# Windowed attention and a gated MLP on one core: q, k and the weights loaded and cast by GpSimd's DMA queue, with all steps in a new order

## The chip, the cores and the metric

The kernel runs on one core of a Trainium2 chip. Its engines are TensorE (PE, with weight loads PEld), VectorE (DVE), ScalarE (ACT), GpSimd (POOL) and SyncE (SP, which here only issues DMAs). The metric is the device time of one execution in microseconds.

## The reference, cut to what matters

Inputs and output are f32. There are 8 batches, 8 heads of 64, a sequence of 576, a model width of 512 and a d_ff of 1024.

```python
scores = q @ k.T / sqrt(64)                       # per batch and head
mask = (rel >= 0) & (rel < 64)                    # rel = row - column
attn = softmax(where(mask, scores, -1e9)) @ v
x = attn.transpose(0, 2, 1, 3).reshape(B, S, 512)

h = maximum(x @ w_in, 0)                          # w_in 512 x 1024
u, v = h[..., :512], h[..., 512:]
v_n = (v - mean(v)) / sqrt(var(v) + 1e-6)
v_s = einsum('ts,bsd->btd', w_spatial, v_n) + b_spatial[None, :, None]
out = (u * v_s) @ w_out                           # w_out 512 x 512
```

## The kernel before, in words

All matmuls are in f16, so every f32 input is cast once on its way. The work is cut into steps. A step has a name, an engine and numbered buffers, and the whole order of the program is a table (ORDER) in which each word is one step: `Vr0_2:ACT:0` is the step Vr0_2 on ACT with buffer 0. Each engine does its own steps in the table's order and waits where an input or a buffer isn't ready; `DQ` in a word is SP's DMA queue. No planner runs when the kernel is built.

Attention goes by batch b and group g of four heads.

- `ldk`, `ldq` (L412) load 576 KB of f32 into a staging buffer (tag `nat`, 8 buffers, shared with the weights); `ck`, `cq` (L289 to L300) cast it to f16 on DVE, ACT or POOL; `tk`, `tq` (L419) transpose it on DVE in 32 x 32 blocks.
- `ldv` (L433) loads v in five pieces with runs of 256 bytes; `cv` casts it, and `sl`, `su`, `s4` (L445 to L458) make a copy that is shifted by 64 rows.
- `S` (L479) are the scores on PE, `E` (L486) their exponential on ACT, `M` (L489) the window mask as a minimum on DVE, `Z` (L502) row sums by a matmul with ones, `P` (L514) the product with v, `N` and `n` (L529, L531) the logarithm of the sums and the exponential of its negative on ACT, `X` (L522) their product with `P` on DVE. Names with `_r` are the same for the last 64 rows.

The MLP goes by batch. `V` and `U` are the two halves of x @ w_in on PE; `Vr` and `Ur` (L669, L763) are their rectifiers on ACT; `Vb`, `Va` (L671, L673) the statistics on DVE; `L1`, `L2` the reciprocal root on ACT; `A` (L728) the normalisation on DVE; `G` the spatial matmul and `Ge` (L797, L800) its product with u on DVE; `O` the output matmul, `Oe` (L647) its copy out of PSUM on ACT, and `st` the store on SP. `W` (L378) transposes w_spatial on PE. `D` (L862) are matmuls on scratch data that only keep PE busy at the start: 27 steps, of which two have nine small matmuls and the others two large ones.

The loads of the weights (`ldwin` L326, `ldwsp` L352, `ldb` L362, `ldwo` L395) go through the same queue and the same staging buffers as q and k, with casts (`cwin`, `cwsp`, `cb`, `cwo`) behind them. The mask and the identity are made first of all on POOL and DVE (L244 to L264). A queue has eight completion semaphores, so the ninth DMA of a queue waits until the first has landed.

Of the kernel before, what the change touches and what calls it, by code (L numbers as in the profile page):

```python
# [18 lines left out]
D24:PE:0 ldb:DQ:0 D5:PE:1 D21:PE:2 ldk0_0:DQ:1 ck0_0:DVE:0 tk0_0:DVE:0 D18:PE:3 D2:PE:2 D14:PE:2  # L19
D19:PE:3 D10:PE:0 ldq0_0:DQ:2 ldk0_1:DQ:3 ldv0_00:DQ:0 ldq0_1:DQ:4 ldv0_10:DQ:1 D3:PE:3 ldv0_11:DQ  # L20
cv0_10:POOL:0 ldk1_0:DQ:5 ck0_1:ACT:1 ldv0_12:DQ ldv0_13:DQ ldv0_01:DQ cq0_0:DVE:2 ldq1_0:DQ:6
tq0_0:DVE:1 ldv0_02:DQ D1:PE:2 S0_0:PE:0:1 tk0_1:DVE:2 D22:PE:0 E0_01:ACT:0 E0_00:ACT:1 cq0_1:DVE:3
tq0_1:DVE:3 D15:PE:3 D6:PE:1 D0:PE:2 D26:PE:0 D23:PE:3 S0_r:PE:1:0 E0_r0:ACT:0 E0_r1:ACT cv0_11:POOL
sl0_10:DVE:0 M0_00:DVE ldv0_03:DQ su0_10:DVE M0_01:DVE ck1_0:DVE:0 M0_r:DVE D8:PE:1 Z0_00:PE:2
ldv0_04:DQ ldwin110:DQ:7 ldv0_14:DQ ldwin111:DQ ldwin100:DQ:1 S0_1:PE:1:0 N0_00:ACT:0 E0_11:ACT:2
D16:PE:0 D7:PE:3 E0_10:ACT:3 M0_11:DVE Z0_01:PE:1 Z0_r:PE:2 D4:PE:0 Z0_11:PE:3 N0_r:ACT:1
N0_01:ACT:2 cv0_00:ACT:1 N0_11:ACT:3 ldwin101:DQ su0_11:DVE M0_10:DVE D12:PE:0 Z0_10:PE:2 D20:PE:1
sl0_11:POOL tk1_0:DVE:4 sl0_00:ACT:1 N0_10:ACT:4 n0_11:ACT n0_10:ACT cq1_0:POOL:2 tq1_0:DVE:5
ldq1_1:DQ:2 ldk1_1:DQ:3 P0_10:PE:0 P0_11:PE:3 cwin110:ACT n0_01:ACT D11:PE:1 cv0_01:POOL
ldwin000:DQ:4 ldwin010:DQ:5 ldwin001:DQ ldwin011:DQ ldwsp1:DQ:6 X0_10:DVE:0 su0_00:DVE X0_11:DVE  # L30
n0_00:ACT sl0_01:POOL cb:POOL su0_01:POOL S1_0:PE:0:1 D25:PE:2 D13:PE:1 P0_00:PE:0 X0_00:DVE:1
E1_01:ACT:3 s40_1:ACT P0_01:PE:2 D9:PE:3 cwin111:POOL cwin100:POOL cwin101:POOL ck1_1:POOL:1
s40_0:ACT E1_00:ACT:2 cwin010:POOL X0_01:DVE cwin001:POOL cwin011:POOL V0_2:PE:1 M1_01:DVE
Vr0_2:ACT:0 n0_r:ACT P0_r:PE:3 Z1_01:PE:0 V0_0:PE:2 ldwsp3:DQ:0 M1_00:DVE N1_01:ACT:5 Vr0_0:ACT:1
cq1_1:DVE:3 Z1_00:PE:1 V0_3:PH:0 V0_1:PE:2 N1_00:ACT:4 cwin000:ACT Vr0_3:ACT:2 Vr0_1:ACT:3
ldwsp0:DQ:7 ldwsp4:DQ:1 ldwsp2:DQ:2 cwsp1:POOL:6 ldv1_00:DQ:2 ldq2_0:DQ:3 X0_r:DVE:0 tq1_1:DVE:7
Vb0_2:DVE:0 V0_4:PE:3 tk1_1:DVE:8 S1_1:PE:1:0 cwsp3:POOL:0 cwsp0:POOL:1 Vb0_0:DVE:1 Vb0_3:DVE:2
Vr0_4:ACT:4 Va0_3:DVE Vb0_4:DVE:3 Va0_4:DVE Va0_0:DVE Va0_2:DVE Vb0_1:DVE:4 Va0_1:DVE U0_2:PH:1
U0_3:PH:0 ldk2_0:DQ:4 U0_4:PE:2 ldv1_01:DQ ldv1_02:DQ ldv1_03:DQ E1_11:ACT:1 E1_10:ACT:0 cwsp2:POOL
cq2_0:POOL:0 M1_10:DVE ldv1_10:DQ:3 Ur0_2:ACT:0 L10:ACT:0 ldv1_11:DQ ldv1_12:DQ ldv1_13:DQ L20:ACT  # L40
ldv1_14:DQ ldq2_1:DQ:5 ldv1_04:DQ ldk2_1:DQ:6 ldwo00:DQ:0 ldwo01:DQ Ur0_4:ACT:1 S1_r:PE:0:1
Z1_10:PE:3 U0_0:PE:1 ldwo10:DQ:7 ldwo11:DQ U0_1:PE:2 E1_r0:ACT:0 Ur0_3:ACT:2 E1_r1:ACT Ur0_0:ACT:3
N1_10:ACT:3 A0_0:DVE:0 A0_3:DVE:1 cwsp4:DVE Ur0_1:ACT:4 W1:PE:0 W3:PE:1 W2:PE:3 W0:PE:2 A0_1:DVE:2
A0_4:DVE M1_11:DVE We1:DVE M1_r:DVE n1_00:ACT We2:ACT We3:ACT A0_2:DVE:3 We0:DVE W4:PE:0 ldq3_0:DQ:1
ldk3_0:DQ:2 ldv2_00:DQ:1 ck2_0:POOL:2 We4:DVE D17:PE:3 Z1_11:PE:1 Z1_r:PE:2 G0_0:PH:3 G0_1:PH:0
tq2_0:DVE:2 n1_10:ACT N1_11:ACT:0 tk2_0:DVE:3 Ge0_0:DVE:0 cv1_00:ACT:2 n1_01:ACT sl1_00:POOL:2
n1_11:ACT su1_00:ACT N1_r:ACT:2 cv1_01:POOL Ge0_1:DVE:1 su1_01:DVE G0_3:PH:1 sl1_01:POOL
cv1_10:ACT:3 Ge0_3:DVE:2 cv1_11:DVE S2_0:PE:0:1 P1_01:PE:2 P1_00:PE:3 X1_00:DVE:2 G0_2:PH:0
sl1_10:POOL:3 ldv2_01:DQ ldv2_02:DQ su1_10:ACT sl1_11:ACT E2_01:ACT:3 n1_r:ACT su1_11:POOL
s41_1:POOL P1_10:PE:1 X1_01:DVE P1_11:PE:3 G0_4:PE:2 X1_10:DVE:3 X1_11:DVE U1_1:PH:1 cq2_1:POOL:3  # L50
E2_00:ACT:2 M2_01:DVE Ur1_1:ACT:5 Ge0_4:DVE:3 ck2_1:POOL:1 ldv2_03:DQ V1_2:PH:3 cwo01:POOL
cwo10:POOL cwo11:POOL Ge0_2:DVE:4 M2_00:DVE Z2_01:PE:2 s41_0:ACT Vr1_2:ACT:5 N2_01:ACT:1 U1_2:PH:1
Ur1_2:ACT:3 P1_r:PE:0 V1_1:PH:3 Vr1_1:ACT:6 cq3_0:POOL:0 Z2_00:PE:2 V1_3:PE:1 tq2_1:DVE:4
# [862 lines left out]
```

## Time and profile before

The time is 195.78 us (median of 3 runs, 195.39 to 196.62). The profiled execution has a span of 193.6 us; the execution time of the runs contains some 2 us beside the span.

| | of the span of 193.6 us |
|---|---|
| PE busy | 184.9 us (95%) |
| DVE busy | 163.7 us (85%) |
| ACT busy | 157.1 us (81%) |
| POOL busy | 87.4 us (45%) |
| SP's queue | 42.04 MB, 73.3% of 16 DMA engines |
| first matmul of the MLP | at 23.42 us |
| last matmul ends | at 189.54 us |

Busy shares are averages over stages of different kinds: about 42 us in which the first batch fills the pipeline, some 147 us in which several batches overlap, and the end. The share of PE also holds the scratch matmuls. What a stage is worth is read from its own windows.

### The profile page before, as it was taken

How to read it: one execution, taken by the hardware profiler on the slowest of the kernel's cores; microseconds unless marked ns; L12 is line 12 of the kernel's file. 1: busy time of each engine (PE TensorE's matmuls, PEld its weight loads, DVE VectorE, ACT ScalarE, POOL GpSimd, SP SyncE). 2: the span in 40 equal slices, each digit the busy share in tenths (PEclk: the TensorE clock that was granted, in tenths of full speed). 3: DMA queues.
4: the chain of work that ended last, by engine and by line, in shares of the span. 5: the costliest groups of instructions: out<-in, count | busy, mean ns of one | idle time of the engine just before them, and what ended most of it. 6: DMA issues, size and time to landing. Idle time of an engine off the chain costs nothing.

```text
span 193.6 us, 7606 instructions
## 1 busy us (share of the span) xinstructions
PE 184.9 (95%) x3218; PEld 107.0 (55%) x3218; DVE 163.7 (85%) x304; ACT 157.1 (81%) x282; POOL 87.4 (45%) x161
## 2 busy tenths in 40 slices
...
PEclk9999999999999999999999999999999999999999
...
GB/s 177 373 316 290 391 355 333 168 275 373 242 205 332 261 335 179 149 38 289 367 230 184 310 310 282 196 177 218 306 125 266 22 3 0 224 30 0 135 166 191
DMA packets 50421, 42.73 MB, mean 221 GB/s; under 512 B 39377, under 2 KB 39761, under 8 KB 50386
## 3 DMA queue, kind: packets, MB, share of 16 engines
q1 hardware_dynamic: 50162, 42.04, 73.3%
q8 instruction: 25, 0.41, 0.9%
q10 hardware_dynamic: 224, 0.20, 0.3%
q14 instruction: 10, 0.08, 0.1%
...
## 4 chain that ended last, share of the span: by engine, by line
PE 70%; DVE 13%; ACT 9%; DMA 3%; issue 2%; SPq 1%
PE bank L617 50%; PE bank L614 4%; PE pair L479 4%; PE bank L514 3%; DMA nk<-in_k_dram 3%; PE bank L502 3%; ACT e L486 3%; DVE qT L419 2%; PE bank L702 2%; DVE e L489 2%; DVE kT L419 2%; DVE st L671 2%; DVE g L797 1%; DVE x L522 1%; ACT lz L529 1%
## 5 line engine op out<-in xcount | busy, mean ns | idle before, releaser
L617 PE MATMUL bank<-wspT,vn 128*64 128x512 f16 (+3 forms) x530 | 39.1, 296 | 0.0
L486 ACT ACTIVATE e<-pair 128x1024 f16<-128x1024 f32 x32 | 32.0, 1030 | 1.6 <-PE pair L479 1.4
L797 DVE TENSOR_TENSOR g<-bank,ru 128x512 f16<-128x512 f32 (+1 forms) x36 | 23.3, 654 | 9.4 <-PE bank L617 7.0
L647 ACT COPY ob<-bank 128x512 f32<-128x512 f32 (+1 forms) x38 | 21.9, 591 | 9.7 <-PE bank L617 8.4
L669 ACT ACTIVATE vs<-bank 128x512 f16<-128x512 f32 (+1 forms) x40 | 23.8, 602 | 7.1 <-PE bank L705 5.6
L617 PE MATMUL bank<-x,win 128*64 128x512 f16 (+2 forms) x304 | 29.1, 327 | 0.0
L617 PEld LDWEIGHTS <-vn 128*64 128x64 f16 (+1 forms) x530 | 20.8, 111 | 13.2 <-issue 0.2
L671 DVE BATCH_NORM_STATS2 st<-vs 128x6 f32<-128x512 f16 (+1 forms) x40 | 26.0, 670 | 2.3 <-ACT vs L669 2.2
L298 POOL COPY hs<-hv 64x512 f16<-64x512 f16 (+1 forms) x36 | 20.1, 585 | 16.3 <-ACT hv L292 8.4
L617 PE MATMUL bank<-win,x 128*64 128x512 f16 x216 | 27.0, 379 | 0.0
L617 PE MATMUL bank<-wout,g 128*64 128x512 f16 (+1 forms) x208 | 24.7, 371 | 0.0
L522 DVE TENSOR_TENSOR x<-bank,lz 128x512 f16<-128x512 f32 x32 | 21.2, 684 | 3.5 <-PE bank L514 2.2
L489 DVE TENSOR_TENSOR e<-e,mask 128x1024 f16<-128x1024 f16 x32 | 23.0, 725 | 0.5 <-ACT e L486 0.4
L763 ACT ACTIVATE ru<-bank 128x512 f32<-128x512 f32 (+1 forms) x38 | 21.6, 584 | 1.5 <-PE bank L617 0.8
L295 POOL CAST hk<-nk 128x384 f16<-128x384 f32 x36 | 19.4, 574 | 7.1 <-DMA nk<-in_k_dram 6.7
L529 ACT ACTIVATE lz<-bank 128x512 f32<-128x512 f32 x32 | 19.0, 599 | 1.9 <-PE bank L502 1.6
L298 POOL CAST hv<-nv 128x512 f16<-128x512 f32 x18 | 11.7, 661 | 18.8 <-DMA nv<-in_v_dram 18.7
L419 DVE STREAM_TRANSPOSE kT<-hk 128x576 f32<-128x576 f32 x16 | 19.9, 1241 | 0.2 <-ACT hk L292 0.2
L419 DVE STREAM_TRANSPOSE qT<-hq 128x576 f32<-128x576 f32 x16 | 19.8, 1237 | 0.2
L531 ACT ACTIVATE lz<-lz 128x512 f32<-128x512 f32 x32 | 19.6, 642 | 0.0
L295 POOL CAST hq<-nq 128x384 f16<-128x384 f32 x27 | 14.9, 588 | 10.3 <-DMA nq<-in_q_dram 7.8
L617 PEld LDWEIGHTS <-win 128*64 128x64 f16 x304 | 14.4, 110 | 9.2
...
## 6 DMA issues: line engine op xcount, KB each, us to landing
...
nv<-in_v_dram SPq DMA_DIRECT2D x64, 128.0 KB, 5.9
...
```

Of the source, the lines that this page charges most:

```text
L295: nc.gpsimd.tensor_copy(o[:, n:n + 384], i[:, n:n + 384])
L298: nc.gpsimd.tensor_copy(o[:, lo:hi, :, :], i[:, lo:hi, :, :])
L419: d = add(f"t{name}{b}_{g}", ("DVE", 1.09), key, lambda e: nc.vector.transpose(qt.t[:, :].rearrange("p (i j) -> p j i", j=18), h.t[:, :].b ...
L486: ex = add(f"E{b}_{g}{u}", ("ACT", 0.91), key, lambda e, u=u: nc.scalar.activation(e2[u].t[:, :, :], sc[u].t[:, :, :], AF.Exp, bias=0.0, s ...
L489: mins.append(add(f"M{b}_{g}{u}", ("DVE", 0.65), key, lambda e, u=u: nc.vector.tensor_tensor(e2[u].t[:, :, :], e2[u].t[:, :, :], mask[:, : ...
L522: lambda e, u=u, ob=ob, lz=lz: nc.vector.tensor_tensor(x.t[:, u, :], ob.t[:, :], lz.t[:, :], ALU.mult),
L617: nc.tensor.matmul(o[c:c + 64, :], w[:, c:c + 64], x, start=start, stop=stop)
L647: lambda e: (nc.vector.tensor_copy if last else nc.scalar.copy)(view(), m.t[rows, 0:n]),
L669: rl = add(f"Vr{b}_{j}", ("ACT", 0.49), key, lambda e: nc.scalar.activation(vs.t[0:jn, :], m.t[0:jn, :], AF.Relu), deps=[pv], acq=[vs], us ...
L671: s1 = add(f"Vb{b}_{j}", ("DVE", 0.6), key + 0.02, lambda e: nc.vector.bn_stats(st6.t[0:jn, 0:6], vs.t[0:jn, :]), deps=[rl], acq=[st6], us ...
L763: lambda e, m=m, ru=ru, n=n: nc.scalar.activation(ru.t[:, 0:n], m.t[:, 0:n], AF.Relu), deps=[pu], acq=[ru], uses=[m])))
L797: nc.vector.tensor_tensor(g.t[:, 0:n], m.t[:, 0:n], ru.t[:, 0:n], ALU.mult)
```

## The change

All loads of k, q, w_in, w_spatial, b_spatial and w_out are issued by GpSimd. Such a transfer has an f32 source and an f16 destination, so the cast takes place on the way, straight into `hqk` (k, q), `win`, `wout`, the rows of w_spatial and row 64 of `wspT`. The staging buffers `nat` and the steps ck, cq, cwin, cwsp, cwo and cb are gone. v and the stores stay on SP, and v keeps its f32 staging and its casts. Making keep, mask, identity and the ones row are now steps of the table (`mkeep`, `mmask`, `mrest`, all on POOL). `Vr`, `Ur` and `Oe` may stand on DVE as well as on ACT (7, 7 and 7 of them do, the one of the last step that was there before among them), and `A` on POOL as well as on DVE (22 of 40 do). Buffer counts change: `natv` 4 to 5, `hqk` 4 to 12, `e2` 4 to 5, `vs` 8 to 10, `ru` 6 to 8. There are 19 steps `D`, each of two large matmuls. The table is new throughout.

```diff
-NWARM, NFILL, FILL = 27, 2, 9
-BUFS = {"nat": 8, "natv": 4, "hqk": 4, "qkT": 9, "hv": 4, "hs": 4, "e2": 4, "er": 1, "lz": 6,
+NWARM = len([w for w in ORDER.split() if w[0] == "D"])
+BUFS = {"natv": 5, "hqk": 12, "qkT": 9, "hv": 4, "hs": 4, "e2": 5, "er": 1, "lz": 6,
...
+    def relu(e, o, i):
+        if e == "ACT":
+            nc.scalar.activation(o, i, AF.Relu)
+        else:
+            nc.vector.tensor_scalar_max(o, i, 0.0)
...
+    MK = [add("mkeep", ("POOL", 0.85), -2.0, make_keep)]
+    MK = [add("mmask", [("DVE", 1.7), ("POOL", 2.0)], -1.9, make_mask, deps=MK)]
+    REST = [add("mrest", ("POOL", 1.9), -1.9, make_rest)]
...
+            for r in range(4):
+                WIN[half, r] = add(
+                    f"ldwin{half}{r // 2}{r % 2}", ("POOL", 0.56), key + 0.01 * (4 * (1 - half) + r),
+                    lambda e, r=r, cs=cs: nc.gpsimd.dma_start(
+                        w_in_sb[r][:, cs], moe_w_in[128 * r:128 * r + 128, cs]), nbytes=0.80, n=128)
...
         def one(name, src, key):
-            n = buf("nat", f"n{name}{b}_{g}")
-            ld = add(f"ld{name}{b}_{g}", ("DQ", 0.45), key, lambda e: nc.sync.dma_start(
-                n.t[:, :], src[b, 4 * g:4 * g + 4, :, :].rearrange("h (i j) d -> (h i) (j d)", j=18)),
-                acq=[n], nbytes=1.57, n=128)
             h = buf("hqk", f"h{name}{b}_{g}")
-            c = add(f"c{name}{b}_{g}", cost(1152), key,
-                    lambda e: cp(e, h.t[:, :], n.t[:, :]), deps=[ld], acq=[h], uses=[n])
+            c = add(f"ld{name}{b}_{g}", ("POOL", 0.56), key, lambda e: nc.gpsimd.dma_start(
+                h.t[:, :], src[b, 4 * g:4 * g + 4, :, :].rearrange("h (i j) d -> (h i) (j d)", j=18)),
+                acq=[h], nbytes=1.57, n=128)
...
-        rl = add(f"Vr{b}_{j}", ("ACT", 0.49), key, lambda e: nc.scalar.activation(
-            vs.t[0:jn, :], m.t[0:jn, :], AF.Relu), deps=[pv], acq=[vs], uses=[m])
+        rl = add(f"Vr{b}_{j}", [("ACT", 0.49), ("DVE", 0.61)], key, lambda e: relu(
+            e, vs.t[0:jn, :], m.t[0:jn, :]), deps=[pv], acq=[vs], uses=[m])
...
-            AP.append(add(f"A{b}_{j}", ("DVE", 0.33), key + 0.2, emit_A,
+            AP.append(add(f"A{b}_{j}", [("DVE", 0.33), ("POOL", 0.7)], key + 0.2, emit_A,
```

**SP's queue at the start.** Before, SP issues the loads of b_spatial (wsb), k (nk), q (nq) and v (nv) of batch 0 and of k and w_in (wi) in turn.

```order
L362 DMA wsb<-in_moe_b_spatial_dram 1x576
L412 DMA nk_0_125<-in_k_dram 128x1152
L412 DMA nq_0_141<-in_q_dram 128x1152
L412 DMA nk_1_143<-in_k_dram 128x1152
L433 DMA nv_0_145<-in_v_dram 128x4x64
L412 DMA nq_1_147<-in_q_dram 128x1152
L433 DMA nv_1_149<-in_v_dram 128x4x64 x2
L412 DMA nk_0_156<-in_k_dram 128x1152
L433 DMA nv_1_149<-in_v_dram 128x4x64 x2
L433 DMA nv_0_145<-in_v_dram 128x4x64
L412 DMA nq_0_165<-in_q_dram 128x1152
```

Now SP issues v alone, and behind v of batch 0 (nv_1_123, nv_0_308) come at once v of batch 1 (nv_1_768, nv_0_875) and of the first group of batch 2 (nv_0_977).

```order
L416 DMA nv_1_123<-in_v_dram 128x4x64 x2
L416 DMA nv_0_308<-in_v_dram 128x4x64
L416 DMA nv_1_123<-in_v_dram 128x4x64
L416 DMA nv_1_123<-in_v_dram 64x4x64
...
L416 DMA nv_0_308<-in_v_dram 64x4x64
L416 DMA nv_1_768<-in_v_dram 128x4x64 x4
L416 DMA nv_0_875<-in_v_dram 128x4x64 x4
L416 DMA nv_1_768<-in_v_dram 64x4x64
L416 DMA nv_0_977<-in_v_dram 128x4x64
```

In the order before, v of batch 1 stood behind all of w_in and w_spatial; now the two kinds of loads stand in different queues, with nothing that holds one for the other.

**POOL at the start.** Before, POOL makes the mask's corner (L244 on), waits for v and casts (hv, hs, hq are v, its shifted copy and q in f16). Now it issues loads (hk, hq are k and q of batches 0 and 1, win is w_in), makes the mask between them, and has two casts of v (the rows hv) in the row, of which the second waits for v of group 0; behind that stand k and q of batch 1's second group and the second half of w_in.

```order
L398 DMA hk_1_129<-in_k_dram 128x1152
L302 MEMSET keep 128x64
...
L398 DMA hq_1_201<-in_q_dram 128x1152
...
L280 CAST hv_1_303<-nv_1_123 128x512 [waits DMAHW1_49,DMAHW0_49]
L358 DMA wspT_100<-in_moe_b_spatial_dram 1x16x36
L398 DMA hq_0_314<-in_q_dram 128x1152
L398 DMA hk_0_316<-in_k_dram 128x1152
L335 DMA win_88<-in_moe_w_in_dram 128x512
...
L280 CAST hv_0_328<-nv_0_308 128x512 [waits DMAHW5_49,DMAHW0_49]
L398 DMA hk_1_370<-in_k_dram 128x1152 [waits DMASW3_49]
```

The casts of k, q and weights are gone from this row, and the loads that other engines wait for now stand in it.

**ACT at the start.** Before (hk is k in f16, e and er the exponentials, lz the sums and their inverses, hv and hs v and its shifted copy, win w_in):

```order
L292 CAST hk_1_158<-nk_1_143 128x1152
L486 ACTIVATE e_0_01_233<-pair_68 128x1024
...
L486 ACTIVATE e_0_11_359<-pair_67 128x1024
L486 ACTIVATE e_0_10_365<-pair_68 128x1024
L529 ACTIVATE lz_r<-bank_71 128x256
L529 ACTIVATE lz_01_383<-bank_70 128x512
L292 CAST hv_0_385<-nv_0_145 128x512
```

Now:

```order
L469 ACTIVATE e_0_10_306<-pair_68 128x1024
L272 CAST hs_1_311<-nv_1_123 64x256
L469 ACTIVATE e_0_11_319<-pair_67 128x1024
L512 ACTIVATE lz_r<-bank_70 128x256
L512 ACTIVATE lz_00_351<-bank_69 128x512
L272 CAST hs_0_332<-nv_0_308 64x256
L272 COPY hs_0_332<-hv_0_328 64x512
L512 ACTIVATE lz_11_375<-bank_72 128x512
```

The cast of k and the casts of w_in are gone; two pieces of v's shifted copy (hs) that need v as it was loaded, and one that needs the cast on POOL (hv_0_328), stand between the exponentials and the logarithms.

**DVE at the end.** Before, the last five products with u (g) stand in a row, and the last copies out of PSUM (ob) behind them:

```order
L797 TENSOR_TENSOR g_2_4828<-bank_70,ru_2_4758 128x512
L797 TENSOR_TENSOR g_3_4871<-bank_69,ru_3_4700 128x512
L800 TENSOR_TENSOR g_4_4896<-bank_72,ru_4_4619 128x256
L835 COPY ob_2_4894<-bank_72 128x256
L647 COPY ob_4_4940<-bank_71 128x256
```

Now the one of the last 64 rows (g_4) comes behind one of those copies:

```order
L780 TENSOR_TENSOR g_0_4769<-bank_71,ru_0_4591 128x512
L780 TENSOR_TENSOR g_3_4773<-bank_70,ru_3_4771 128x512
L818 COPY ob_2_4796<-bank_70 128x256
L783 TENSOR_TENSOR g_4_4862<-bank_69,ru_4_4467 128x256
L818 COPY ob_2_4796<-bank_72 128x256
```

On PE the last spatial matmul, G7_4, moved with it: before it directly followed G7_3, now three output matmuls and half of a fourth stand between them, and G7_3 is followed at once by output matmuls.

More of the change, by code (lines that the diff above doesn't have):

```diff
@@ L18 @@
 ORDER = """
[L19 to L53, printed above, removed]
@@ new lines @@
+ldv0_14:DQ ldq1_0:POOL:4 ldk1_0:POOL:5 s40_1:ACT E0_11:ACT:3 ldv0_03:DQ ldv0_13:DQ ldwin100:POOL
+ldwin111:POOL ldv0_01:DQ su0_10:DVE cv0_11:DVE cv0_00:DVE:1 ldv0_02:DQ M0_10:DVE sl0_00:DVE:1
+M0_11:DVE ldwin101:POOL ldv0_04:DQ su0_00:DVE tq1_0:DVE:4 su0_11:DVE Z0_00:PE:0 Z0_r:PE:1 N0_r:ACT:0
+N0_00:ACT:1 ldwin110:POOL cv0_01:POOL Z0_01:PE:2 D16:PE:3 D17:PE:3 D18:PE:3 Z0_11:PE:3 Z0_10:PE:1
+ldk1_1:POOL:6 sl0_01:POOL s40_0:ACT su0_01:ACT N0_11:ACT:2 n0_00:ACT N0_01:ACT:3 N0_10:ACT:4
+sl0_11:POOL n0_r:ACT P0_01:PE:0 P0_00:PE:3 tk1_0:DVE:5 P0_11:PE:2 ldq1_1:POOL:7 ldwin000:POOL
```

322 lines of the change are left out of this document (159 added, 163 removed).

## The prediction

> **What bounds the kernel now.** I read the page's totals first, then the stages by windows, then TensorE's row of instructions around the stages' borders.
>
> ```profile
> span 193.6 us, 7606 instructions
> PE 184.9 (95%) x3218; PEld 107.0 (55%) x3218; DVE 163.7 (85%) x304; ACT 157.1 (81%) x282; POOL 87.4 (45%) x161
> ...
> PEclk9999999999999999999999999999999999999999
> ```
>
> PE is busy for 95% of the span, and the clock row shows no throttled slice. The windows (us, busy time of PE, PEld, DVE, ACT and POOL, clock, DMA share, GB/s) say where the other 5% lie.
>
> ```profile
> 0.00:9.26 9.26, 6.87 (x21) 2.53 (x22) 6.05 (x16) 2.34 (x2) 2.31 (x11) 1.00 0.78 275
> 9.26:23.42 14.16, 13.17 (x298) 6.76 (x298) 13.29 (x19) 11.82 (x21) 8.60 (x13) 1.00 1.11 329
> 23.42:42.04 18.62, 17.75 (x214) 8.73 (x215) 17.82 (x34) 17.22 (x35) 12.47 (x19) 1.00 0.97 282
> 42.04:189.54 147.50, 147.12 (x2689) 88.95 (x2687) 126.48 (x237) 125.33 (x226) 64.00 (x118) 1.00 0.69 201
> 189.54:193.60 4.06, 0.00 (x0) 0.00 (x0) 0.08 (x1) 0.37 (x1) 0.00 (x0) 1.00 0.54 169
> ```
>
> From 42.04 to 189.54 PE is busy for 147.12 of 147.50 us, and none of it is scratch work (all steps D lie before). PE bounds this stage; DVE, ACT and POOL have 21 us and more to spare in it. The change takes no matmul of the result away, so these 147.1 us stay, and faster casts are worth nothing there. What can move is the first 42 us, where PE's busy time is filled up with scratch matmuls and the DMA engines are full, and the last few.
>
> ```profile
> 1.27 6.87 PE L862 MATMUL bank<-scratch 128*128 128x512 f16 x20 [1.27 <-DVE scratch L237]
> ...
> 13.89 0.67 PE L479 MATMUL pair<-qT,kT 32*128 32x128 f16 x56
> ...
> 23.42 0.39 PE L614 MATMUL bank<-win,x 128*128 128x512 f16 x1
> 24.02 0.82 PE L614 MATMUL bank<-win,x 128*128 128x512 f16 x3 [0.21 <-DVE x L522]
> ...
> 29.85 0.67 PE L479 MATMUL pair<-qT,kT 32*128 32x128 f16 x56 [0.42 <-DVE kT L419]
> 30.45 1.92 PE L617 MATMUL bank<-x,win 128*64 128x512 f16 x16
> 32.30 0.64 PE L614 MATMUL bank<-x,win 128*128 128x64 f16 x16
> ...
> 35.48 2.39 PE L378 MATMUL bank<-id,wn 128*128 128x128 f16 x25
> 37.80 0.61 PE L862 MATMUL bank<-scratch 128*128 128x512 f16 x2
> ...
> 38.69 3.42 PE L617 MATMUL bank<-wspT,vn 128*64 128x512 f16 x30
> ```
>
> Two marks: 23.42, when the first V may start because the attention of batch 0 is done, and 42.04, from where PE is never short. Between them PE has, by distances of starts, nine groups V and U at about 0.9 (30.45 to 32.30 is two: 1.85), U0_4 0.57, W 2.32 (35.48 to 37.80), three G 3.35 (38.69 to 42.04), S1_1 0.60, and Z, S_r, P_r and Z_r at some 1.2 together: about 16 of 18.62 us. So about 2.7 us of that stage is waiting, scratch work included.
>
> **The change part by part, the start.** What stands ahead of 23.42 is a chain of DMA, cast, transpose, scores, exponential. DVE's rows, then ACT's:
>
> ```profile
> 5.26 0.76 DVE L300 CAST hk<-nk 128x1152 f16<-128x1152 f32 x1 [1.66 <-DMA nk<-in_k_dram]
> 6.06 1.26 DVE L419 STREAM_TRANSPOSE kT<-hk 128x576 f32<-128x576 f32 x1
> 7.16 0.75 DVE L300 CAST hq<-nq 128x1152 f16<-128x1152 f32 x1
> ...
> 10.49 0.74 DVE L300 CAST hq<-nq 128x1152 f16<-128x1152 f32 x1
> ...
> 22.67 1.29 DVE L522 TENSOR_TENSOR x<-bank,lz 128x512 f16<-128x512 f32 x2 [0.18 <-PE bank L514]
> ...
> 25.60 1.06 DVE L300 CAST hq<-nq 128x1152 f16<-128x1152 f32 x1
> ```
>
> ```profile
> 8.20 1.15 ACT L292 CAST hk<-nk 128x1152 f16<-128x1152 f32 x1 [6.11 <-DMA nk<-in_k_dram]
> ...
> 14.79 1.94 ACT L486 ACTIVATE e<-pair 128x1024 f16<-128x1024 f32 x2 [0.20 <-PE pair L479]
> ...
> 17.51 0.61 ACT L292 CAST hv<-nv 128x512 f16<-128x512 f32 x1
> 18.02 0.61 ACT L529 ACTIVATE lz<-bank 128x512 f32<-128x512 f32 x1
> 18.65 0.40 ACT L292 COPY hs<-hv 64x256 f16<-64x256 f16 x1
> ...
> 20.61 0.61 ACT L292 CAST win<-wi 128x512 f16<-128x512 f32 x1
> 21.12 1.15 ACT L531 ACTIVATE lz<-lz 128x512 f32<-128x512 f32 x2
> 22.17 1.01 ACT L486 ACTIVATE e<-pair 128x1024 f16<-128x1024 f32 x1
> 23.20 0.71 ACT L292 CAST hs<-nv 64x256 f16<-64x256 f32 x2
> ```
>
> Gone ahead of S0_1 are three casts on DVE (0.76, 0.75, 0.74) and one on ACT (1.15). The four loads, not DVE, then set the pace. SP's issue rows:
>
> ```profile
> 1.21 0.38 SPq L412 DMA_DIRECT2D nk<-in_k_dram  x1
> ...
> 6.14 3.98 SPq L433 DMA_DIRECT2D nv<-in_v_dram  x3
> ...
> 27.08 0.43 SPq L433 DMA_DIRECT2D nv<-in_v_dram  x1
> ```
>
> The first k needed 4.05 us from its issue at 1.21 to its cast at 5.26. What an issue by GpSimd costs the trace does not show. Bounds: SP's 0.38 below, and above the 1.33 that SP's v rows took apiece when the queue was full (3.98 for 3). I take the middle, 0.8, since a row on the engine itself is nearer to compute. Nor is a transfer with a cast shown: below, its time is that of the plain one (half the bytes written); above, it is twice, which is a rival. With plain speed the four 576 KB loads (2.36 MB) share the DMA engines with v of batch 0, which now has a queue to itself. At 329 GB/s of the window, 2.36 MB and half of v's 1.18 take 9.0 us; from about 2 us on that is 11.0 for the fourth load. The transpose (a distance of 1.1 in DVE's rows, 6.06 to 7.16) ends near 12.1, and S0_1 follows near 13.4, against 13.89. The distance before was 1.5 (the cast at 10.49, 0.74 and 1.1 make 12.4), with Z0_00 and its wait for M0_00 ahead of S0_1; that goes, and I take 1.3, since S0_r and its exponentials stay.
>
> From S0_1 to E is 0.90 (13.89 to 14.79), so E starts at 14.3. Before, ACT's list from there to the last inverse took 7.38 (14.79 to 22.17). Out of it go cv 0.51 (17.51 to 18.02), sl 0.40 and cwin 0.51 (20.61 to 21.12); into it come two pieces s4 of 0.37 (half of 23.20's pair, rounded up), su at 0.51 as cv, and n_r at half of what one n takes in 21.12's pair, 0.3: 7.5. Then the last X takes 0.65 (22.67's two at 1.29), and V may have run up to 0.55 of its four matmuls before it: 14.3 + 7.5 + 0.65 - 0.55 = 21.9. To that I add 1.3 of stalls: ACT's two s4 and su stand in front of logarithms and wait for v and POOL's cast, and DVE's cv0_11 and cv0_00 wait for v in front of M0_10 and M0_11. Bounds of this term: 0, if v comes first, and 2.5, worked out under the rivals. The mark comes to **23.2 instead of 23.42: -0.2**.
>
> Of the work between the marks, P_r (0.13) and V0_4 (0.88) now stand ahead of V0_3 and fall into ACT's time: **-1.0**. Of 2.7 us of waiting, the transposes of k1_1 and q1_1 no longer stand behind the cast of 1.06 at 25.60 (PE waited 0.42 for it at 29.85), and the casts of w_spatial between the load and W are gone; waits for the statistics and for A0_1, now on POOL, stay. I take 1.3 left, **-1.4**; bounds 0.5 and 2.7.
>
> **The rest.** Of ACT's 157 us, casts, 14 rectifiers and copies go, some 23; DVE loses and gains about as much; POOL trades 35 casts for 22 A and 50 issues. In the long stage all that is covered by PE: at nothing, while buffers keep their lead. If POOL ran late with A, G would wait: A costs 0.42 on DVE, and on POOL between 0.6 and 1.1, as POOL's cast rows of the same elements:
>
> ```profile
> 11.50 0.61 POOL L300 CAST hv<-nv 128x512 f16<-128x512 f32 x1 [8.33 <-DMA nv<-in_v_dram]
> 14.08 0.92 POOL L300 CAST hv<-nv 128x512 f16<-128x512 f32 x1 [1.97 <-DMA nv<-in_v_dram]
> ```
>
> Four A, two on POOL at 0.9, are ready about as early as five at 0.42. The end:
>
> ```profile
> 185.11 0.69 DVE L797 TENSOR_TENSOR g<-bank,ru 128x512 f16<-128x512 f32 x1 [0.39 <-PE bank L617]
> ```
>
> G7_4 used to run while DVE did the last Ge7_3 of 0.69; now O7_0 follows G7_3 and waits for earlier Ge. The other O7 cover part. I take **+0.5**, between 0 and 0.7. The copy and store after the last matmul are the same: the last window's 4.06.
>
> Sum: 193.6 - 0.2 - 1.0 - 1.4 + 0.5 = 191.5 of span. The median of 195.78 lies 2.2 above the profiled span: 193.7, which I give as 193.6.
>
> A rule of the Trainium skill speaks against the change. The row first: the two casts on POOL above are alike, and the second took 0.92 instead of 0.61 beside a DVE cast, so the two engines do hold each other up, by 0.31. The Trainium skill ("SBUF — State Buffer", SBUF: two separate sides) says that DVE's fast copy modes lock GpSimd out of a port pair, so that it can't write the descriptors of its DMAs meanwhile, and gives 620 ns growing to 3100 ns for such a DMA. By that rule each load issued beside such a DVE copy would come later by up to the copy; no run here shows it for a load.
>
> **The rivals.** *First, v comes late (no change).* v has 256-byte runs, and its queue now competes with big transfers. For: v rows took 1.33 of issue each at a full queue, and the DMA share is 1.11 in that window. Against: v has no k, q or weights ahead of it in its own queue now. Then the stall is 2.5 instead of 1.3 (two pieces of v's 1.18 MB at half of 329 GB/s more, 0.2 MB: 1.2), and POOL's cv0_01 holds k1_1, q1_1 and w_in's second half behind it, so that 0.7 less of the waiting goes: 193.6 + 1.2 + 0.7 = 195.5.
>
> *Second, v of batches 1 and 2 comes first (slower).* SP now issues 1.77 MB of v right behind batch 0's, which before came at 27.08, behind w_in and w_spatial. The start is full: 1.11 and 0.97 of the DMA engines. At 320 GB/s 1.77 MB take 5.5 us. If a share f of it gets ahead of w_in's second half and w_spatial, U0 and W wait by 5.5 f, less some 0.5 of slack that U0 has. 193.6 + 5.5 f - 0.5 is even with before at f = 0.5, over 1% slower from 0.84, and 198.6 at f = 1. For: nothing but the eight semaphores holds SP back. Against: those let only eight v pieces be under way, and each of 128 KB landed 5.9 us after issue. The Trainium skill ("DMA: Bandwidth & Descriptors", Queues, rings and completion order) says that a DMA engine takes its queues in turn, a packet from each; by that rule f would be large, since v's queue never empties early.
>
> ```profile
> nv<-in_v_dram SPq DMA_DIRECT2D x64, 128.0 KB, 5.9
> ```
>
> *Third, loads with a cast are slow (slower).* At half speed, k, q and weights (23.6 of 42 MB) would raise the long stage's share from 0.69 to 0.69 x (1 + 23.6 / 42) = 1.08: DMA would bound it, and 8% of 147.5 is 12 us: 205. Held up for less, it gives 200. Against: 12 buffers for k and q give three batches of lead.
>
> **How the numbers follow.** Within 1% (193.8 to 197.7) is what this kernel's measurement can't tell from no change. The forecast case gets 0.50; its bounds make it 191.0 to 195.2, and since 193.6 is near the border, 0.36 of it is faster, 0.14 the same. The first rival gets 0.22 (0.05, 0.14, and 0.03 slower), the second 0.19 (0.05 the same, 0.14 slower), the third 0.09, all slower. That is 0.41, 0.33 and 0.26. The range 191.2 to 198.6 leaves out the third rival, 0.03 above the second and 0.06 below.
>
> **What would show it.** Right: V starts at about 23.2 with fewer scratch matmuls, PE has no gap from some 39.5 on, and the last matmul ends 2 us earlier. First rival: ACT's hs or DVE's hv rows idle for v. Second: U's first matmuls wait for win, or W for w_spatial, behind landings of v. Third: GpSimd's loads land much later after their issue than the first k's 4.05 and v's 5.9, and k's transposes wait in the long stage. The forecast is wrong if PE waits for A on POOL in the long stage.

## The result, and the profile after

The changed kernel takes 232.01 us (median of 4 runs, 229.82 to 240.53) against 195.69 us (195.39 to 196.62): a ratio of 1.1735, with a 95% interval of 1.1691 to 1.1778. The forecast was 193.6, with a range to 198.6. All ratios below go by the runs within 1.5% of their kernel's fastest, so a median over all runs can lie above its ratio.

The page of the changed kernel, beside the one of before: the span is 34.1 us longer. PE is idle for 36.7 us of it instead of 8.7. Its matmuls on real data, the same in both kernels, take 180.0 us instead of 168.8 (the mean granted clock is 0.962 instead of 1.000), and the scratch matmuls take 10.9 instead of 16.1.

```profile
span 227.7 us, 7662 instructions
## 1 busy us (share of the span) xinstructions
PE 191.0 (84%) x3295; PEld 110.4 (48%) x3295; DVE 163.0 (72%) x288; ACT 138.3 (61%) x249; POOL 124.7 (55%) x171
...
PE   7591898599995999599957999976999799499692
...
PEclk9999599979999999999997999997999999999999
```

PE's row had a 9 in nearly every slice before; now it has 4, 5 and 7 all along the span, and behind some of them the granted clock is lowered. Its windows say that this is not a matter of the start alone (us, busy time of PE, PEld, DVE, ACT and POOL, clock, DMA share, GB/s).

```profile
0.00:42.00 42.00, 31.41 (x463) 16.10 (x463) 27.11 (x50) 22.21 (x39) 22.68 (x47) 0.92 0.97 178
42.00:60.00 18.00, 15.01 (x311) 8.94 (x312) 14.47 (x21) 12.56 (x23) 16.66 (x27) 0.91 0.76 121
60.00:180.00 120.00, 106.13 (x1984) 63.62 (x1980) 98.54 (x173) 86.19 (x155) 74.65 (x94) 0.97 0.65 144
180.00:230.00 50.00, 38.41 (x548) 21.75 (x542) 22.90 (x48) 17.37 (x34) 10.77 (x5) 0.97 0.24 83
```

In the long stage, which had 0.38 us of idle time in 147.5 before, PE is idle for 13.9 of 120 us between 60 and 180. Over the whole span, the waits name one cause for more than half of the idle time (us in total, times, longest):

```profile
PEld L600 <- POOL vn L711: 24.7, 11, 4.2
PE bank L600 <- POOL vn L711: 20.3, 11, 3.7
```

L711 is the normalisation A, and L600 here the spatial matmul G, which reads all five tiles of a batch. The row of L711 by engine (ns: least, median, most):

```profile
L711 POOL TENSOR_SCALAR vn<-vs,mv,ln x22: 2062/2069/2720, 38.4 to 211.9; 128x512 f16<-128x512 f16 x18, 64x512 f16<-64x512 f16 x4
L711 DVE TENSOR_SCALAR vn<-vs,mv,ln x18: 396/413/806, 38.3 to 210.7; 128x512 f16<-128x512 f16 x14, 64x512 f16<-64x512 f16 x4
```

On POOL an A takes 2.07 us, five times DVE's 0.41. Its least and its median are alike, so this is its own price and no disturbance by DVE. POOL as a whole is busy for only 55% of the span: G waits not because POOL is full, but because the last A of a batch ends late. Batch 0 shows it, on POOL's timeline and then on PE's:

```profile
20.74 1.09 POOL L280 CAST hv<-nv 128x512 f16<-128x512 f32 x1 [8.93 <-DMA nv<-in_v_dram]
...
38.45 2.23 POOL L711 TENSOR_SCALAR vn<-vs,mv,ln 128x512 f16<-128x512 f16 x1 [5.01 <-ACT ln L701]
40.64 0.62 POOL L398 DMA_DIRECT2D hq<-in_q_dram  x1
41.31 4.25 POOL L711 TENSOR_SCALAR vn<-vs,mv,ln 64x512 f16<-64x512 f16 x2
```

```profile
10.70 0.67 PE L462 MATMUL pair<-qT,kT 32*128 32x128 f16 x56 [2.48 <-DVE qT L402]
...
16.29 1.47 PE L844 MATMUL bank<-scratch 128*128 128x512 f16 x6
22.69 1.07 PE L485 MATMUL bank<-e,ones 128*64 128x512 f16 x4 [4.93 <-DVE e L472]
...
28.02 0.64 PE L600 MATMUL bank<-win,x 128*64 128x512 f16 x1
...
45.62 2.28 PE L600 MATMUL bank<-wspT,vn 128*64 128x512 f16 x48 [2.79 <-POOL vn L711]
```

Batch 0's three A on POOL run from 38.45 to 45.56, with a load of q between them. Two matmuls of G0 run at 42.44; the others wait until 45.62. There is a second, smaller loss ahead of it: v of batch 0's second pieces (group 0) is there only at 20.7 (POOL's cast waited 8.93 us for it). DVE's casts of v stand in front of M0_10, so PE is idle for 4.93 us before the next row sums; the matmuls behind that pause run at 0.63 us where the same ones took 0.38 before, in the slices whose granted clock is 5 and 9. The scores began at 10.70 instead of 9.26, the first V at 27.6 instead of 23.42.

### The profile page after: what moved, and what is told of

The parts are those of the page before. It is cut to its first block, busy times and chain, and to the rows that moved or that the text cites. A ratio compares the mean times of both kernels' runs of the same rounds, so it can differ in the third digit from the quotient of the medians.

```text
span 227.7 us, 7662 instructions
## 1 busy us (share of the span) xinstructions
PE 191.0 (84%) x3295; PEld 110.4 (48%) x3295; DVE 163.0 (72%) x288; ACT 138.3 (61%) x249; POOL 124.7 (55%) x171
## 3 DMA queue, kind: packets, MB, share of 16 engines
q1 hardware_dynamic: 43168, 18.68, 31.8%
q0 software_dynamic: 7024, 11.68, 30.7%
## 4 chain that ended last, share of the span: by engine, by line
PE 32%; POOL 19%; SPq 11%; DVE 11%; issue 10%; DMA 8%; ACT 6%; POOLq 1%; DVEq 0%; ACTq 0%
PE bank L600 24%; POOL vn L711 18%; SPq L416 10%; DMA nv<-in_v_dram 8%; DVE x L505 2%; PE bank L685 2%; PE pair L462 2%; PE bank L497 2%; DVE g L780 1%; DVE st L654 1%; ACT lz L512 1%; PE bank L485 1%; DVE qT L402 1%; DVE e L472 1%; DVE kT L402 1%
## 5 line engine op out<-in xcount | busy, mean ns | idle before, releaser
L711 POOL TENSOR_SCALAR vn<-vs,mv,ln 128x512 f16<-128x512 f16 (+1 forms) x22 | 47.9, 2181 | 62.5 <-ACT ln L701 47.9
L600 PE MATMUL bank<-wspT,vn 128*64 128x64 f16 (+3 forms) x640 | 48.3, 303 | 20.4 <-POOL vn L711 20.3
L600 PEld LDWEIGHTS <-vn 128*64 128x64 f16 (+1 forms) x640 | 25.3, 121 | 39.8 <-POOL vn L711 24.7
L469 ACT ACTIVATE e<-pair 128x1024 f16<-128x1024 f32 x32 | 32.2, 1026 | 15.6 <-PE pair L462 15.5
L600 PE MATMUL bank<-win,x 128*64 128x512 f16 x240 | 31.8, 383 | 0.2 <-DVE x L505 0.2
L600 PE MATMUL bank<-x,win 128*64 128x512 f16 (+2 forms) x352 | 31.7, 317 | 0.1
L600 PE MATMUL bank<-wout,g 128*64 128x512 f16 (+1 forms) x240 | 28.8, 373 | 0.2
L272 ACT COPY ob<-bank 128x512 f32<-128x512 f32 (+2 forms) x34 | 19.3, 580 | 14.3 <-PE bank L600 9.8
L284 ACT ACTIVATE vs<-bank 128x512 f16<-128x512 f32 (+1 forms) x33 | 19.3, 595 | 10.2 <-PE bank L600 3.0
L284 ACT ACTIVATE ru<-bank 128x512 f32<-128x512 f32 (+1 forms) x31 | 17.8, 586 | 11.5 <-PE bank L600 11.3
L472 DVE TENSOR_TENSOR e<-e,mask 128x1024 f16<-128x1024 f16 x32 | 22.6, 715 | 0.0
L600 PEld LDWEIGHTS <-win 128*64 128x64 f16 x352 | 16.2, 110 | 10.4 <-issue 0.8
L600 PEld LDWEIGHTS <-x 128*64 128x64 f16 x240 | 14.1, 110 | 11.4 <-DVE x L505 1.1
L600 PEld LDWEIGHTS <-g 128*64 128x64 f16 x240 | 13.9, 110 | 10.4 <-DVE g L780 1.0
```

What stands on the lines that cost most here:

```text
L284: nc.scalar.activation(o, i, AF.Relu)
L469: ex = add(f"E{b}_{g}{u}", ("ACT", 0.91), key, lambda e, u=u: nc.scalar.activation(e2[u].t[:, :, :], sc[u].t[:, :, :], AF.Exp, bias=0.0, s ...
L472: mins.append(add(f"M{b}_{g}{u}", ("DVE", 0.65), key, lambda e, u=u: nc.vector.tensor_tensor(e2[u].t[:, :, :], e2[u].t[:, :, :], mask[:, : ...
L600: nc.tensor.matmul(o[c:c + 64, :], w[:, c:c + 64], x, start=start, stop=stop)
L711: ENG[e].tensor_scalar(o[0:jn, :], VS[j].t[0:jn, :], mv_t[b % NSB][0:jn, j, 0:1], ln.t[0:jn, 5 + j:6 + j], ALU.subtract, ALU.mult)
```

## The experiments

Three explanations were to be told apart: the price of A on POOL; the loads, now in two queues; and the new order as such.

**A back on DVE, in the changed kernel.** All 22 words, of this kind:

```diff
-A0_2:POOL:0
+A0_2:DVE:0
```

> The changed kernel with one edit: the 22 normalisations A that stand on POOL go back to DVE, at the same places in the order. Theory 1 (A on POOL is the main cost: 2.07 us each there against 0.41 on DVE, and TensorE's rows wait 20.3 + some 5 us for it): the time falls from 232 by 25 to 32 us, to 200 to 207, and TensorE no longer waits for vn. Theory 2 (the loads at the start and v's late arrival are the main cost): it falls by less than 12 us, to over 220. Theory 3 (the new order as a whole is bad, wherever A stands): over 215, with the waits spread over other rows.

208.5 us, ratio 1.0595 (1.0513 to 1.0678). The fall from 1.1735 is 0.114, some 22 us of the 34: the first theory's direction, a little less than its numbers. 12 us are left.

**A on POOL, in the kernel before.** The same 22 steps:

```diff
-A0_2:DVE:3
+A0_2:POOL:3
```

> The kernel before with one edit: the same 22 normalisations A go from DVE to POOL, at their places in the order before. Theory 1: it slows by 20 us or more, to 215 to 230, since each A takes about 2.1 us on POOL and G waits for the last of a batch. Theory 2: DVE is relieved and POOL had time to spare, so under 200. It also shows whether A's 2.07 us come with POOL's loads: about 2.07 here too if the operation itself costs that, under 1.1 if issuing loads was what slowed it.

229.4 us, ratio 1.1709 (1.1621 to 1.1797). Alone, with nothing else of the change, A on POOL costs as much as the whole change did. The rows of A in this kernel:

```profile
L728 POOL TENSOR_SCALAR vn<-vs,mv,ln x22: 2064/2068/2720, 37.5 to 214.7; 128x512 f16<-128x512 f16 x18, 64x512 f16<-64x512 f16 x4
L728 DVE TENSOR_SCALAR vn<-vs,mv,ln x18: 312/402/791, 33.9 to 213.5; 128x512 f16<-128x512 f16 x14, 64x512 f16<-64x512 f16 x4
```

The 2.07 us are there without a single load issued on POOL, so issuing has nothing to do with it. 22 times the difference of 1.66 is 36.5 us, near the 33.4 that were added, but the time isn't added up tile by tile: in this trace PE's idle time goes from 8.7 to 31.1 us, and its busy time from 184.9 to 198.4 for the same matmuls, at a mean granted clock of 0.937. In the changed kernel the same 22 steps were worth some 22 us.

**What in A is slow on POOL.** One run of the changed kernel with other forms in four batches:

```diff
+                if e == "POOL" and b == 1:
+                    nc.gpsimd.tensor_scalar(o[0:jn, :], i_, m_, None, ALU.subtract)
+                elif e == "POOL" and b == 2:
+                    nc.gpsimd.tensor_scalar(o[0:jn, :], i_, 0.5, 2.0, ALU.subtract, ALU.mult)
+                elif e == "POOL" and b == 3:
+                    nc.gpsimd.tensor_scalar(o[0:jn, :], i_, 2.0, None, ALU.mult)
+                elif e == "POOL" and b == 4:
+                    nc.gpsimd.tensor_copy(o[0:jn, :], i_)
```

> The changed kernel, in which A on POOL has another form in some batches, to price its parts: batch 1 only subtracts (one operand per row), batch 2 subtracts and multiplies by constants, batch 3 multiplies by a constant, batch 4 copies; the others as they were, at 2.07. So the normalisation of batches 1 to 4 is in part left out here, and the time is read only by these rows. If the two operands per row are what costs, batch 2 is near the 0.6 of POOL's copies; if two operations on POOL cost that, batch 2 is near 2.07 and batches 1 and 3 near 1.1; if any tensor with scalars is slow, batch 3 is far over the copy of batch 4.

The rows by form (L721 as it was, L713 batch 1, L715 batch 2, L717 batch 3, L719 batch 4; ns: least, median, most):

```profile
L721 POOL TENSOR_SCALAR vn<-vs,mv,ln x12: 2061/2072/2684, 37.5 to 204.0; 128x512 f16<-128x512 f16 x9, 64x512 f16<-64x512 f16 x3
L717 POOL TENSOR_SCALAR vn<-vs x3: 1501/1626/1802, 109.3 to 113.0; 128x512 f16<-128x512 f16 x2, 64x512 f16<-64x512 f16 x1
L719 POOL COPY vn<-vs x3: 611/612/617, 133.1 to 137.1; 128x512 f16<-128x512 f16 x3
...
L713 POOL TENSOR_SCALAR vn<-vs,mv x2: 1560/1568/1577, 66.3 to 67.9; 128x512 f16<-128x512 f16 x2
L715 POOL TENSOR_SCALAR vn<-vs x2: 1920/1988/2057, 79.2 to 81.2; 128x512 f16<-128x512 f16 x2
```

The third guess is right, by two or three tiles of each form: a tensor with scalars is slow on POOL as such, 1.5 to 1.8 us with one operation and 1.9 to 2.1 with two, whether the scalars are constants or one per row, where a copy of the same tile takes 0.61.

**v of batches 1 and 2 held back, A on DVE.** v of batch 1 uses batch 0's staging buffers, and its words stand behind the casts that free them:

```diff
-ldv1_10:DQ:2 ... ldv1_00:DQ:3
+ldv1_10:DQ:0 ... ldv1_00:DQ:1
```

> The changed kernel with A on DVE as in the first run of this group, and v of batches 1 and 2 held back: v of batch 1 uses the staging buffers of batch 0 and its loads stand behind the casts that free these, with v of batch 2's first group behind them. If v ahead of time takes the bandwidth from v of batch 0's second group, w_in and w_spatial at the start (V began some 4 us later than before in the changed kernel), it is 3 to 5 us faster than the run with A on DVE alone, and the first V starts at about 24 instead of about 28. If the bandwidth of the start isn't what is short, it is within 1 us of that run, or slower, because v of batch 1 then comes late.

209.7 us, ratio 1.0673 (1.0609 to 1.0737): no gain. POOL's cast shows why:

```profile
20.95 1.09 POOL L280 CAST hv<-nv 128x512 f16<-128x512 f32 x1 [8.99 <-DMA nv<-in_v_dram]
```

v of batch 0 is as late with nothing behind it in its queue. The second rival of the prediction, v ahead of its time, is not it.

**v of batch 0 first, A on DVE.** POOL's cast cv0_01, which waits for v, goes ahead of six loads:

```diff
+cv0_01:POOL ldq1_0:POOL:4 ldk1_0:POOL:5 ldwin100:POOL ldwin111:POOL ldwin101:POOL ldwin110:POOL
```

> A on DVE as before this, and one more edit: GpSimd issues k and q of batch 1's first group and the first half of w_in only behind its cast of v of batch 0's second pieces, so these 2.2 MB no longer share the DMA engines with v of batch 0. In the runs with A on DVE v of batch 0 was there at about 20.4 us, with or without v of batch 1 behind it. If the loads of the other queue hold v back, v is there at about 14 to 16, DVE's cast of it waits less, the first V starts 3 to 4 us earlier than 27.4 and the time falls from 208.5 to about 204 to 206. If v's own 256-byte runs or SP's issue set its time, v stays near 20 and the time rises by the later w_in, to 210 to 213.

205.07 us, ratio 1.0441 (1.0362 to 1.0520). POOL's timeline and PE's:

```profile
14.31 0.83 POOL L280 CAST hv<-nv 128x512 f16<-128x512 f32 x1 [6.44 <-DMA nv<-in_v_dram]
15.10 0.57 POOL L398 DMA_DIRECT2D hq<-in_q_dram  x1
```

```profile
18.77 0.62 PE L485 MATMUL bank<-e,ones 128*64 128x512 f16 x4 [1.21 <-DVE e L472]
...
24.81 1.04 PE L685 MATMUL bank<-win,x 128*64 128x512 f16 x2
```

v comes 6 us earlier, PE waits 1.21 instead of 4.93, and the first V starts at 24.8 instead of 27.4. In time that is 3.4 us by the medians (the two intervals just touch). So k and q of batch 1 and w_in, 2.2 MB that are needed later, had taken the DMA engines from v: with two queues the order in which loads were issued no longer is the order in which they land.

**The rectifiers and copies back on ACT.** On top of that, the 19 steps of this kind:

```diff
-Vr0_4:DVE:0
+Vr0_4:ACT:0
```

> The run with A on DVE and v of batch 0 first, with one more edit: the 19 rectifiers and output copies of batches 0 to 7 that the change put on DVE go back to ACT, at the same places. That run is still some 9 us slower than before, with TensorE idle for some 3.5 us between 60 and 180 us (0.3 before) and no cast left on DVE but v's. If the work put on DVE (each about 0.65 there) is what delays others in its row, the idle time falls below 1.5 us and the time by 2 to 4 us, to 201 to 203. If the rows' order as such is what costs, it stays at 204 to 206; if ACT's row can't take it, over 206.

208.03 us, ratio 1.0521 (1.0452 to 1.0590): no gain. Relieving DVE alone doesn't mend the new order. Whether DVE's load costs nothing, or ACT, with 19 steps more, loses what DVE gains, this run doesn't tell.

**The new order with A on POOL at the price of a copy.** POOL's 22 A are plain copies; in the second run v of batch 0 comes first as well.

```diff
+                if e == "POOL":
+                    nc.gpsimd.tensor_copy(o[0:jn, :], VS[j].t[0:jn, :])
+                    return
```

> The changed kernel with POOL's 22 normalisations replaced by plain copies of the same size (0.61 us each in the run of the forms, against 2.07), everything else and every place in the order kept: the new order at the price that the prediction took for A on POOL. The normalisation of these 22 tiles is left out, and with it POOL's wait for the batch's statistics, so this is the best that the order could do. If the price of A is what failed, the time is at most that of the run with A on DVE, 203 to 208. If A's place in POOL's row, behind loads and casts that wait, costs besides, it is 212 or more.

> The same with v of batch 0 first, as in the run with A on DVE and v first (205). If what is left there (some 9 us over before) comes from A standing on DVE, which the new order had not left room for, this comes to 195 to 199; if the new order is slow by itself, 201 to 205, with TensorE's idle time between 60 and 180 us still at 2 us or more.

205.11 us, ratio 1.0382 (1.0297 to 1.0468), and 202.06, ratio 1.0333 (1.0278 to 1.0388). At the price of a copy, and without the wait for the batch's statistics, A on POOL costs no more than on DVE (1.0382 against 1.0595, and 1.0333 against 1.0441 with v first). And yet the new order is 3.3% slower than the old one at its best. The windows from 60 us on, of the run with A on DVE and v first, then of the second one here, then of the kernel before:

```profile
60.00:180.00 120.00, 116.61 (x2216) 72.74 (x2212) 110.86 (x208) 89.65 (x161) 42.03 (x71) 1.00 0.63 142
180.00:230.00 50.00, 17.25 (x202) 9.43 (x198) 7.89 (x18) 7.61 (x15) 0.00 (x0) 0.96 0.17 58
```

```profile
60.00:180.00 120.00, 118.44 (x2237) 77.10 (x2235) 107.13 (x194) 90.77 (x166) 51.77 (x89) 1.00 0.63 143
180.00:230.00 50.00, 15.10 (x182) 9.39 (x178) 7.10 (x15) 6.55 (x14) 0.00 (x0) 0.98 0.17 58
```

```profile
60.00:180.00 120.00, 119.67 (x2172) 72.63 (x2161) 105.42 (x198) 104.86 (x189) 52.81 (x98) 1.00 0.66 189
180.00:230.00 50.00, 9.54 (x136) 5.89 (x130) 3.95 (x7) 4.02 (x8) 0.00 (x0) 0.98 0.15 48
```

Between 60 and 180 us that is 3.4 and 1.6 us of idle time, against 0.3 before. But the greater part is lost earlier. The matmuls that are left at 60 us take 133.9 and 133.5 us (116.61 + 17.25 and 118.44 + 15.10), against 129.2 before. So of the 7.8 us by which the first span is longer (201.4), 4.7 are lost before 60 us, and of the 5.7 of the second (199.3), 4.3.

**The loads alone.** The order before, with the loads of k, q and weights by GpSimd at their old places, without their casts:

```diff
-ldk0_0:DQ:1 ck0_0:DVE:0 tk0_0:DVE:0
+ldk0_0:POOL:0 tk0_0:DVE:0
```

> The loads alone: the order before, with all rectifiers, copies and normalisations on their engines, but k, q and the weights loaded and cast by GpSimd in the places where their loads stood, the casts gone, 12 buffers for k and q, and the mask made on POOL between the first loads. If casting in the transfer costs no transfer time (the changed kernel's trace: 69.9 us of all 16 engines for these loads, as many as the difference of the two kernels' rows gives for before), and v ahead costs little, 192 to 196. If v of batch 1 ahead of w_in and w_spatial costs at the start, 197 to 201. If issuing on POOL holds POOL up, over 201, with waits for POOL's casts and copies of v in the long stage.

199.96 us, ratio 1.0131 (1.0044 to 1.0219). Its longest wait of PE in the first 42 us is one that the rewriting made, POOL's shifted copies of v standing behind eight issues:

```profile
26.72 0.26 PE L498 MATMUL bank<-e,hs 128*64 128x64 f16 x2 [3.19 <-POOL hs L281]
```

From 60 us on this run is as full as the kernel before:

```profile
60.00:180.00 120.00, 119.65 (x2209) 72.22 (x2205) 104.31 (x196) 103.54 (x190) 42.65 (x74) 1.00 0.62 145
180.00:230.00 50.00, 14.53 (x182) 8.55 (x176) 7.76 (x19) 6.87 (x15) 0.00 (x0) 0.97 0.15 48
```

134.2 us of matmuls are left at 60, against 129.2 before. That is all of the 5.0 us by which its span is longer (198.6).

So these copies were put ahead, and identity and ones earlier:

```diff
+cv0_01:POOL sl0_01:POOL su0_01:POOL ldwin000:POOL ldwin010:POOL
```

> The loads alone, in the order before, with one place mended: POOL makes identity and ones early, where it waits for v anyway, and makes the shifted copies of v of group 0 right behind its cast, ahead of the second half of w_in and w_spatial. In the first run of the loads alone TensorE waited 3.5 us for these copies, which stood behind eight issues. If that wait was what made it 4 us slower than before, 196 to 197; if it is v's late arrival (20.8 us) and w_in's (issued from 16.9 on), 199 to 201, with the wait moved to win or v.

Ratio 1.0028 (0.9987 to 1.0069): at its best, no change. But the ten runs lie between 195.24 and 201.11, with a median of 198.27, where the kernel before has 195.92. The kept trace is of the run of 201.11. PE's timeline, and a window:

```profile
10.22 0.67 PE L463 MATMUL pair<-qT,kT 32*128 32x128 f16 x56 [2.34 <-DVE qT L403]
...
23.77 0.39 PE L598 MATMUL bank<-win,x 128*128 128x512 f16 x1
...
47.70 0.27 PE L498 MATMUL bank<-e,hs 128*64 128x64 f16 x2 [2.64 <-ACT hs L273]
```

```profile
42.00:60.00 18.00, 14.87 (x296) 8.64 (x286) 12.16 (x21) 10.87 (x18) 4.15 (x8) 0.81 0.82 162
```

The scores begin 1 us later than before and the first V 0.35 later, though three casts on DVE and some on ACT are gone. But the scores that stand at 42.04 before start at 41.80 here, so up to there nothing is lost. What this run loses, it loses next: v of batch 1, in SP's queue, is late. DVE's cast of it waits 3.90 us, until 46.57, PE waits 3.1 us in two pieces for the shifted copies, and its granted clock is 0.81 in the window. So a queue that is left to v alone doesn't bring v in time here, which is the second case of the expectation. Whether the other runs of this kernel that took longer lost their time there too, no trace shows.

**All loads of the start in one queue.** v of batches 0 and 1 by GpSimd too:

```diff
-                           lambda e, c=c, sn=sn: nc.sync.dma_start(
+                           lambda e, c=c, sn=sn: ENG[e].dma_start(
```

> The loads alone with all loads of the start in one queue: v of batches 0 and 1 is issued by GpSimd too, at the places that its loads had in SP's queue before, the mask is made on DVE, and POOL's first casts of v stand behind the issues. If it is the second queue that breaks the order in which loads arrive, v of batch 0 is there by about 14, the first V starts near 24 and the time is 195 to 198. If GpSimd's way of loading is itself late (the first k took 5.4 us from its issue instead of 4.05) or its issues of v with 512 runs each cost POOL far more than 0.55, the scores start no earlier than 10.4 and the time is 200 or more.

202.8 us, ratio 1.0258 (1.0216 to 1.0300). It answers another question than it was made for. In the kept trace, of the run of 209.10, the scores began at 9.30, as early as before. But POOL was busy with 18 issues, and waits between them for loads to land, until its first cast of v at 17.76. On DVE a shifted copy waited for this cast, with the product with the mask (M) behind it, and PE waited 6.04 us for M.

```profile
20.03 0.64 PE L487 MATMUL bank<-e,ones 128*64 128x512 f16 x2 [6.04 <-DVE e L474]
```

An issue of v took 0.75 there, one of k or q 0.55. Whether one queue brings v in time can't be told from it: the last piece of v of batch 0 was issued only at 17.13, after POOL had waited 1.55 us for an earlier one to land.

**A mixture.** The order before; k and q of batch 0 by SP with casts, all other k and q and the weights by GpSimd:

```diff
+            if b == 0:
+                n = buf("nat", f"n{name}{b}_{g}")
+                ld = add(f"ld{name}{b}_{g}", ("DQ", 0.45), key, lambda e: nc.sync.dma_start(n.t[:, :], rows),
+                         acq=[n], nbytes=1.57, n=128)
...
+            else:
+                c = add(f"ld{name}{b}_{g}", ("POOL", 0.56), key,
+                        lambda e: nc.gpsimd.dma_start(h.t[:, :], rows), acq=[h], nbytes=1.57, n=128)
```

> A mixture meant to beat the kernel before: its order, with k and q of batch 0 loaded by SP and cast on DVE and ACT as before, and k and q of the other batches and all weights loaded and cast by GpSimd, with POOL's row mended as in the run with the shifted copies first. In the runs with the loads alone the first scores began about 1 us later than before (10.2 against 9.26), since GpSimd's first loads land later, and the first V 0.35 us later, though ACT had three casts less ahead of it. If the late first loads are the only price of the loads, this starts V at 22.8 to 23.2 and gives 194.5 to 195.3, 0.3 to 0.7% faster than before. If v and w_in are as late as in those runs, it is the same as before, 195.5 to 197.

194.84 us (12 runs), ratio 0.9940 (0.9916 to 0.9964): 0.6% faster than the kernel before, which is little but clear of the noise. PE's timeline and the long stage:

```profile
8.68 0.67 PE L471 MATMUL pair<-qT,kT 32*128 32x128 f16 x56 [1.43 <-DVE qT L411]
...
22.85 0.39 PE L606 MATMUL bank<-win,x 128*128 128x512 f16 x1
```

```profile
60.00:180.00 120.00, 119.65 (x2159) 72.55 (x2156) 103.13 (x196) 101.27 (x185) 43.25 (x74) 1.00 0.61 142
```

The first V starts 0.57 earlier than before, as the expectation had it. That is most of the 0.7 us between the profiled spans (192.9 against 193.6), and the stage from 60 to 180 is as full as before: the casts that went gave about 1 us, all of it ahead of 60 us.

## Why the prediction was wrong

**What bounds the kernel** was read rightly: PE bounds the long stage, and the loads alone (ratio 1.0028) and the mixture (0.9940) show that removing casts is worth nothing there (PE is busy for 119.7 of 120 us between 60 and 180 in all three) and little at the start.

**The step that failed** is this one: "A costs 0.42 on DVE, and on POOL between 0.6 and 1.1, as POOL's cast rows of the same elements", and with it "at nothing, while buffers keep their lead". The bound was taken from another operation with as many elements. A measured 2.07 on POOL, and a copy of the same tile 0.61; G waits for the slowest tile, and A on POOL alone turns the kernel before into one of 229.4 us. Of the change's 34 us some 22 are this. The sentence that four A, two on POOL, are ready about as early as five on DVE went with it: batch 0's two last A on POOL alone took 4.25. The prediction did name PE waiting for A on POOL as what would make it wrong, but gave it no price and no chance; with an open upper end for an operation that the trace did not show on that engine, it should have been a rival of its own.

**The start.** The forecast had V at 23.2; it was 27.6. The issue by GpSimd was taken at 0.8 and measured 0.53 to 0.62, after 0.73 for the first. The first k was there 5.5 us after its issue (4.05 before), and the fourth load at 12.6 instead of the 11.0 worked out. So S0_0 was late, S0_1 came at 14.6 instead of 13.4, and E at 15.6 instead of 14.3: 1.3 of the 4.4 us. The other 3.1 make the stall some 4.4 instead of 1.3, if the rest of that sum held. It was the size that failed most: PE alone was idle for 4.93, and then ran at a lowered clock. The first rival had the right mechanism, v coming late behind the other queue's loads, but its 2.5 was too small by almost half. Between the marks, 2.7 us of waiting was read too high: the window of 23.42 to 42.04 shows PE idle for 0.87 us, and one scratch step of 0.61 ran in it, so no more than 1.5 could go.

**The second rival**, v of batches 1 and 2 ahead of its time, fell: holding it back gained nothing (1.0673 against 1.0595). Its sign, U waiting for w_in and W for w_spatial, shows in PE's rows of the changed kernel with 0.7 and 0.2 us only. The Trainium skill's rule beside it ("DMA: Bandwidth & Descriptors", Queues, rings and completion order), that a DMA engine takes its queues in turn, fits what happened the other way round: with GpSimd's later loads under way, v of batch 0 landed 6 us later. The turns themselves no view here shows.

**The third rival**, loads with a cast at half speed, fell by the rows of the queues, of before and then of after (packets, MB, share of 16 engines):

```profile
q1 hardware_dynamic: 50162, 42.04, 73.3%
```

```profile
q1 hardware_dynamic: 43168, 18.68, 31.8%
q0 software_dynamic: 7024, 11.68, 30.7%
```

SP's queue took 73.3% of 193.6 = 141.9 us before and 31.8% of 227.7 = 72.4 after, so k, q and the weights took 69.5 us of all engines before, if v and the stores took as much then as now; GpSimd's queue, which now carries them, took 30.7% of 227.7 = 69.9. (11.68 MB is counted in f16.) By these rows a cast in the transfer costs no transfer time. The kernel is slower in the range that this rival would have reached, for another reason.

**The rule of the Trainium skill** that was weighed ("SBUF — State Buffer", SBUF: two separate sides) says that DVE's copies can hold up GpSimd's descriptors. Here an issue of k, q or weights took 0.53 to 0.73 of POOL's time, also beside a busy DVE, and k and q landed 6.6 and 6.5 us after their issue (medians; 6.6 and 6.1 by SP before). No run singles out such a delay.

**The tail** was put at +0.5. In the changed kernel, by its timeline, PE's weight loads wait 0.37 and 0.61 for the last products with u, and 0.42 for the one of the last 64 rows. PE's own rows show how much was not covered. From the first of G7_4 and O7 to the end of the last matmul it was 4.7 us before (184.83 to 189.54) and is 5.4 now (218.44 to 223.83): +0.7, the upper bound.

**What stays open.** With A and v mended, the new order is still 4.4% slower than the old one, with POOL's A at the price of a copy 3.3%. The loads in the old order cost 0.3% at their best and 1.2% by the median of all their runs. What the two runs above lose after 60 us, 3.1 and 1.4 us, is idle time of PE that the loads alone don't have: so much is the new order's. It isn't shown which of its rows: moving the rectifiers back did not help (1.0521), DVE is busy for 110.9 of 120 us (105.4 before), and the idle time is spread over many short waits. The greater part, 4.7 and 4.3 us, is lost before 60 us. There the loads and the order act together, and the loads alone lost 5.0 and 5.8 us in their kept traces, so the two are not told apart. A run with the order before up to some step and the new one behind it wasn't tried.
